# An fp32 block of layernorm, attention and MLP on one core: the maxima's hand-over, W_V's low parts and 19 matmuls of zeros

## The chip, the core and the metric

The kernel runs on one core of one Trainium2 chip. A core has a matrix engine (TensorE, PE in the profile; PEld is its weight load), VectorE (DVE), ScalarE (ACT), GpSimd (POOL) and SyncE (SP). SP and ACT issue the DMAs of this kernel, each into a queue of its own (SPq and ACTq in the profile). The metric is the device time of one execution in microseconds (us); lower is better, and the median of several runs is compared.

## The reference, cut to what matters

```python
S, D, H, F = 2048, 1024, 32, 3584           # head size 32, everything in float32
xn = layernorm(x)                            # over D, eps 1e-5, no weights
q, k, v = split(xn @ wqkv)
o = softmax(q @ k.T / sqrt(32)) @ v          # for each of the 32 heads
s = o @ wo
h = xn @ w1 + b1
g = silu((h * tanh(softplus(h))) @ w2)       # mish between two dense layers
return x + s * g
```

## The kernel before

**Precision.** Every float32 operand of a large product is split into a high part (rounded to the PE's fp32r form) and a low part (the difference). A product is three matmuls: high by high, high by low and low by high (`THREE`). Each split costs one copy for the high part (`copy`, line 288, on ACT) and one subtraction for the low part (`low`, line 296, on DVE or POOL). So one line of a helper stands for many operations in the profile.

**Stages.** The first stage normalises x and projects V (lines 371 to 642). A second projects Q and K with a seven-product scheme (lines 645 to 864; line 795 is its matmul). From about 522 us on, attention and MLP run together under a planner (lines 867 to 1451), and the last stage applies `wo` and adds up.

**The start.** x is taken in 16 tiles of 128 rows. `ln_a` is the statistics (lines 391 to 394, DVE), `ln_r` two small ACT operations, `ln_b` four small DVE operations (lines 404 to 407), `ln_x` the normalisation. For the first three tiles `ln_x` is shared: the first half on ACT (line 413), the second on DVE (line 416). `ln_t` makes eight PE transposes into two PSUM banks (line 423), and `ln_c` copies each bank to the tile's high part (ACT) and takes its low part (DVE). `v_group(0, t)` is the 24 matmuls of one x tile with the first half of W_V (line 354): eight row blocks k, three matmuls each. A group stops after `cut` matmuls to put the next tile's transposes in. The first group takes the pairs that need only W_V's high parts first, 16 matmuls, and the eight with its low parts last. The order of the instructions on each engine is the order in which lines 469 to 531 are written. `v_high(0, k)` and `v_low(0, k)` make the parts of W_V's eight blocks; blocks 4 and 5 have their low parts made by POOL, the others by DVE.

**The hand-over to attention.** The softmax subtracts each row's maximum by two extra rows of the Q stack (high and low part of the negated maximum). The scores of head 0 are computed ahead, during the Q and K projection (`s_mm`); their maxima are reduced by DVE. The first twelve of 16 row tiles are turned on the way (`m_tail`). The last four go through `m_chain(0, 12, 4)`, the first thing that the planner has:

- r1: the maximum over four chunks (DVE, line 937)
- r2: high part (ACT, line 940)
- r3: low part (DVE for head 0)
- r4: `turn`, a matmul with the identity (PE, line 678)
- r5: copy from PSUM (ACT, line 952)
- r6: two small DMAs into rows 96 and 97 of the Q stack (line 957). For head 0 they are issued on ACT's queue, for the others on SP's.

Head 0's exponentials of key tile t need `t` matmuls (line 999), which read the Q stack with those rows; the fourth chunk of queries waits for r6.

**The planner.** `Plan` simulates the engines with written-out costs and emits each instruction at the simulated time at which its engine would take it. That order is then the program order of each engine's queue. It has streams of PE work: `s` (scores for maxima, line 917), `t`, `h` (first MLP product, line 1204), `y` (second, line 1294), `pv`. Op by op it holds a cost, an engine and what must be done first; what an op really emits is a function of its own, which the planner doesn't look into.

**Weights.** Tile n of W1 (1 MB, high and low part) is loaded by `load_w1(n)` into one of two buffers. Tile 0 is loaded at the end of the projections, tile 1 by `w1_op(1)`, whose op on SP the planner emits among the first there, ahead of r6. W2's first raw tile (line 1160) is given `m_there[0, 3]`, the op of r6, as a need (line 1281), so it is emitted after it.

Of the kernel before, what the change touches and what calls it, by code (L numbers as in the profile page):

```python
# [9 lines left out]
F32 = mybir.dt.float32  # L10
# [8 lines left out]
P = 128  # L19
# [211 lines left out]
def body(ctx: ExitStack, tc: tile.TileContext, x, wqkv, wo, w1, b1, w2, out):  # L231
# [99 lines left out]
    def v_high(i, k):  # L331
        j, k = divmod(k, 2)
        if k == 0:
            vw[i, j] = vp.tile([P, 2, 2, 512], F32R, tag="w", name=f"vw{i}_{j}", bufs=5)
        copy(vw[i, j][:, 0, k], vraw[i, j][:, k])

    def v_low(i, k, eng):
        j, k = divmod(k, 2)
        low(eng, vw[i, j][:, 1, k], vraw[i, j][:, k], vw[i, j][:, 0, k])
# [40 lines left out]
    def ln_a(t, steps=range(3)):  # L380
        xt = xts[t]
        if 0 in steps:
            st = vp.tile([P, 2, 6], F32, tag="st", name=f"st{t}", bufs=4)
            mv = vp.tile([P, 2], F32, tag="mv", name=f"mv{t}", bufs=5)
            var = vp.tile([P, 1], F32, tag="var", name=f"var{t}", bufs=5)
            rs = vp.tile([P, 1], F32, tag="rs", name=f"rs{t}", bufs=5)
            stat[t] = mv, var, rs, st
        mv, var, rs, st = stat[t]
        for g in range(2):
            if g in steps:  # L390
                nc.vector.bn_stats(st[:, g], xt[:, g * 512:(g + 1) * 512])
        if 2 in steps:
            nc.vector.bn_aggr(mv, st)
            nc.vector.tensor_scalar(var, mv[:, 1:2], EPS, None, op0=ALU.add)

    def ln_r(t):
        mv, var, rs, _ = stat[t]
        act(rs, var, AF.Ln)
        act(rs, rs, AF.Exp, scale=-0.5)
# [66 lines left out]
        move(xs[c][:, :, k:k + 2], xc[c][k // HK][:, :, k % HK:k % HK + 2])  # L466


    ln_a(0)
    ln_r(0)  # L470
    ln_b(0)
# [8 lines left out]
    ln_c(0)  # L480
    ln_a(1, (1, 2))
    v_low(0, 2, nc.vector)
    v_high(0, 3)
    v_low(0, 3, nc.vector)
    for k in (4, 5):
        v_high(0, k)
        v_low(0, k, nc.gpsimd)
    v_high(0, 6)
    v_high(0, 7)
    ln_r(1)  # L490
    v_low(0, 6, nc.vector)
    ln_b(1)
    ln_x(1, True)
    v_low(0, 7, nc.vector)
    ln_a(2)
    xts[3] = x_load(3)
    for t in range(2, NT + 2):
        if 2 < t < NT:
            ln_b(t)

        evac = v_group(0, t - 2, {2: 22, 3: 20, 4: 14}.get(t, 8), (lambda: ln_t(t - 1)) if t <= NT else None,
                       (((0, 0), (1, 0)), ((0, 1),)) if t == 2 else None if t > NT else (((0, 0), (0, 1)), ((1, 0),)))
        if t <= NT:
            ln_c(t - 1)
        if t == 2:
            ln_r(2)
            ln_b(2)
        if t < NT:
            ln_x(t, t == 2)
        for m in (4, 5) if t == 2 else (t + 3,):  # L510
            if m < NT:
                xts[m] = x_load(m)
        if t == 2:
            ln_a(3)
        if t + 2 < NT:
            ln_a(t + 2)
        if t + 1 < NT:
            ln_r(t + 1)
        if t in (NT - 4, NT - 3):
            for j in range(2):  # L520
                v_load(1, 2 * (t - NT + 4) + j)
        if t == NT - 2:
            v_split(1, 0)
        if t == NT + 1:
            for j in range(1, 4):
                v_split(1, j)
        evac()
        if t in (8, 10, 12, 14, 17):
            x_store()
        if t in (4, 5, 7, 9, 11, 13, 15):  # L530
            w1_early()
# [401 lines left out]
    def m_chain(h, first, n, maxes, tiles):  # L933

        def r1(at):
            tiles["nm"] = early.tile([P, NT], F32, tag=f"nm{at['nm']}", name=f"nm{h}_{first}")[:, :n]
            nc.vector.tensor_reduce(tiles["nm"], tiles["mx"][:, :n], axis=AX.X, op=ALU.max, negate=True)

        def r2(at):
            copy(parts(n)[:, 0], tiles["nm"])  # L940

        def r3(at):
            hl = parts(n)
            low(nc.vector if h == 0 else nc.gpsimd, hl[:, 1], tiles["nm"], hl[:, 0])

        def r4(at):
            tiles["tp"] = tp = bank(at, f"mtp{h}_{first}")
            turn(tp)

        def r5(at):  # L950
            tiles["mt"] = early.tile([2 * NT, P], F32R, tag=f"mt{at['mt']}", name=f"mt{h}_{first}")
            copy(tiles["mt"][:2 * n], tiles["tp"][:2 * n, :P])

        def r6(at):
            for a in range(2):
                move(qst[h % 3][96 + a:97 + a, first * P:(first + n) * P]
                     .rearrange("o (t p) -> o t p", p=P), tiles["mt"][n * a:n * a + n, :], None if h else nc.scalar)

        a = op("DVE", 0.18, need=maxes, emit=r1, take=["nm"], give=["mx"])
        a = op("ACT", 0.21, need=[a], emit=r2, take=["hl"])  # L960
        a = op("POOL" if h else "DVE", 0.25, need=[a], emit=r3, give=["nm"], key=-1)
        a = op("PE", 0.07, need=[a], emit=r4, take=["t", "b"], give=["hl"], late=LATE if h else 0.0)
        a = op("ACT", 0.28, need=[a], emit=r5, take=["mt"], give=[("t", a), ("b", a)])
        a = op("SP", 0.2, need=[a], emit=r6, give=["mt"], bytes_=1024 * n)
        for c in range(first // 4, (first + n) // 4):
            m_there[h, c] = a
# [145 lines left out]

    def w1_op(n):
        def emit(at):
            load_w1(n)
        need = [w1_kept.get(n - 2)]
        if not W1_V <= n < FT:
            w1_ops[n, 0] = w1_ops[n, 1] = op("SP", 0.1, need=need, emit=emit, take=["w1"], bytes_=P * 2 * KT * P * 4)
            return
        a = None  # L1120
        for half in range(2):
            r = slice(half * HK, half * HK + HK)

            def raw(at, half=half):
                if half == 0:
                    w1t[n] = w1_tile(f"w1_{n}")
                w1r[n, half] = att.tile([P, 512], F32, tag="on0", name=f"w1r_{n}_{half}").rearrange("p (k f) -> p k f", f=P)
                nc.sync.dma_start(w1r[n, half], w1[half * 512:half * 512 + 512, n * P:(n + 1) * P].rearrange("(k p) f -> p k f", p=P))

            def high(at, half=half, r=r):  # L1130
                copy(w1t[n][:, 0, r], w1r[n, half])

            def rest(at, half=half, r=r):
                low(nc.gpsimd, w1t[n][:, 1, r], w1r[n, half], w1t[n][:, 0, r])

            b = op("SP", 0.1, need=[a] + need, emit=raw, take=["on"] if half else ["w1", "on"], bytes_=P * 512 * 4)
            a = op("ACT", 0.6, need=[b], emit=high)
            w1_ops[n, half] = op("POOL", 1.3, need=[a], emit=rest, give=["on"], key=-1)
        w1_kept[n] = op("SP", 0.1, emit=lambda at: move(w1s[n], w1t[n]), need=[w1_ops[n, 0], w1_ops[n, 1]], bytes_=P * 2048 * 4)
# [412 lines left out]
```

## Time and profile before

| what | us |
|---|---|
| median of 3 runs | 3364.82 |
| lowest and highest of them | 3362.99, 3366.28 |
| the profiled execution's own time | 3366.45 |
| its span, first to last instruction | 3364.7 |
| PE busy | 3342.9 |
| DVE, ACT, POOL busy | 2511.9, 2056.0, 2527.5 |

How to read the rows. The page gives each engine's busy time with its share of the span, and the chain of work that ended last, as shares by engine. A row of the timeline has the start in us, the duration in us, the engine, the line, the operation, output and inputs by their names, the shape and a count; in brackets stands how long the engine sat idle before it, and what ended the wait. Rows of several instructions are merged, and matmuls overlap: one lasts longer than the distance to the next. A row of the view by stretches has the length, then for PE, PEld, DVE, ACT and POOL the busy time with a count, then the granted PE clock, the share of the DMA engines and the GB/s that they moved. A row of the view by line has the least, median and largest duration in ns, and the first and last start.

### The profile page before, as it was taken

The numbers are of one execution on the slowest core, as the hardware profiler recorded it, in microseconds if no ns is written. First come the engines' busy times: TensorE is split into PE (matmuls) and PEld (weight loads), VectorE is DVE, ScalarE is ACT, GpSimd is POOL, SyncE is SP. The second block draws the span as 40 slices with busy tenths as digits, with TensorE's granted clock in tenths as the row PEclk, the third lists the DMA queues.
The fourth block names the chain that finished last, engine by engine and source line by source line (L and its number), as shares of the span: only waits on it lengthen the run. The fifth ranks groups of instructions, "written<-read, shape, count | busy, mean of one in ns | idle before, by whom it ended". The sixth has DMA issues, their size and how long they took to land.

```text
span 3364.7 us, 45751 instructions
## 1 busy us (share of the span) xinstructions
PE 3342.9 (99%) x16867; PEld 2455.6 (73%) x16867; DVE 2511.9 (75%) x3984; ACT 2056.0 (61%) x3314; POOL 2527.5 (75%) x751
## 2 busy tenths in 40 slices
PE   8999999999999999999999999999999999999999
PEld 7888887777777677776777667777677777767787
DVE  6665677878777777887788678888787888886542
ACT  5233335777766666676676666667667666667621
POOL 2323546999999977888888988888888898889800
PEclk9999999999999999999999999999999999999999
DMA  7865745454555643344335434333344433433482
GB/s 242 302 204 180 242 145 180 144 179 153 168 188 176 208 135 116 104 123 121 101 113 164 129 101 126 101 103 117 108 151 136 119 104 111 128 111 107 138 305 83
DMA packets 291460, 501.56 MB, mean 149 GB/s; under 512 B 88138, under 2 KB 151114, under 8 KB 269130
## 3 DMA queue, kind: packets, MB, share of 16 engines
q1 hardware_dynamic: 271508, 456.95, 43.7%
q10 hardware_dynamic: 19728, 41.69, 3.3%
q8 instruction: 133, 2.18, 0.3%
q14 instruction: 91, 0.75, 0.1%
HBM read 352.55 MB, written 144.97 MB: 148 GB/s over the span
## 4 chain that ended last, share of the span: by engine, by line
PE 95%; DMA 2%; DVE 1%; POOL 1%; issue 0%; ACT 0%; SPq 0%; ACTq 0%; DVEq 0%; POOLq 0%
PE y L1294 18%; PE h L1204 17%; PE t L999 14%; PE s L917 13%; PE pv L1046 13%; PE op L1393 5%; PE v L354 5%; PE q_y L795 3%; PE q_z L795 2%; PE q_x L795 2%; PE zp L1072 1%; POOL z L1028 1%; DMA raw<-in_A_wqkv_dram 0%; PE pt L423 0%; PE s L697 0%
## 5 line engine op out<-in xcount | busy, mean ns | idle before, releaser
L1028 POOL TENSOR_TENSOR z<-z,p 128x2048 f32<-128x2048 f32 x448 | 2068.3, 4617 | 98.1 <-ACT p L285 72.8
L285 ACT ACTIVATE p<-t,zero 128x512 f32<-128x512 f32 x2048 | 1377.0, 690 | 564.2 <-PE t L999 539.7
L923 DVE TENSOR_REDUCE mx<-s 128x1 f32<-128x512 f32 x1984 | 1323.7, 686 | 385.7 <-PE s L917 374.5
L1294 PE MATMUL y<-w,act 128*128 128x512 f32 x2688 | 920.7, 391 | 1.1 <-DVE yacc L1316 0.5
L999 PE MATMUL t<-qstack,kstack 128*128 128x512 f32 x2048 | 800.0, 393 | 4.1 <-DMA qstack<-mt 3.3
L917 PE MATMUL s<-kstack,qstack 128*128 128x512 f32 x1984 | 773.1, 394 | 0.0
L1204 PE MATMUL h<-xr,w 128*128 128x512 f32 x2016 | 697.6, 391 | 0.4 <-DMA xr<-xs 0.4
L1294 PEld LDWEIGHTS y<-w,act 128*128 128x128 f32 x2688 | 503.3, 188 | 115.0 <-issue 6.7
L999 PEld LDWEIGHTS t<-qstack,kstack 128*128 128x128 f32 x2048 | 384.1, 188 | 118.7 <-issue 20.9
L1046 PE MATMUL pv<-p,v 128*32 128x512 f32 x4096 | 459.3, 594 | 0.0
L917 PEld LDWEIGHTS s<-kstack,qstack 128*128 128x128 f32 x1984 | 370.0, 188 | 118.4 <-issue 32.1
L1204 PEld LDWEIGHTS h<-xr,w 128*128 128x128 f32 x2016 | 378.3, 188 | 81.2 <-issue 3.4
L1316 DVE TENSOR_TENSOR yacc<-yacc,y 128x512 f32<-128x512 f32 x416 | 283.0, 681 | 82.3 <-PE y L1294 81.4
L1046 PEld LDWEIGHTS pv<-p,v 128*32 128x32 f32 x4096 | 123.3, 110 | 282.8 <-issue 282.2
L1028 POOL TENSOR_TENSOR z<-p,p 128x2048 f32<-128x2048 f32 x32 | 148.1, 4628 | 185.5 <-PE zp L1072 142.1
L1204 PE MATMUL h<-xc,w 128*128 128x512 f32 x672 | 231.8, 392 | 0.3 <-ACT p L285 0.3
L354 PE MATMUL v<-vw,xc 128*128 128x512 f32 x768 | 180.4, 394 | 0.0
L354 PEld LDWEIGHTS v<-vw,xc 128*128 128x128 f32 x768 | 143.9, 189 | 30.3 <-DVE xc L296 0.5
L1204 PEld LDWEIGHTS h<-xc,w 128*128 128x128 f32 x672 | 126.2, 188 | 29.3 <-issue 2.5
L288 ACT ACTIVATE act<-h 128x512 fp32r<-128x512 f32 x112 | 66.6, 595 | 88.3 <-DVE h L1253 87.1
L795 PE MATMUL q_y<-xc,wq 128*128 128x512 f32 x480 | 115.4, 389 | 0.0
L795 PEld LDWEIGHTS q_y<-xc,wq 128*128 128x128 f32 x480 | 90.0, 188 | 18.9 <-issue 0.2
(146 smaller groups left out, 2940.3 us busy)
## 6 DMA issues: line engine op xcount, KB each, us to landing
w<-w1s SPq DMA_DIRECT2D x91, 1024.0 KB
w<-w2s SPq DMA_DIRECT2D x168, 512.0 KB
w2s<-w SPq DMA_DIRECT2D x56, 512.0 KB
qstack<-qs SPq DMA_DIRECT2D x96, 256.0 KB
kstack<-ks SPq DMA_DIRECT2D x96, 256.0 KB
w1s<-w SPq DMA_DIRECT2D x21, 1024.0 KB
qs<-qst ACTq DMA_DIRECT2D x32, 512.0 KB
ks<-qst ACTq DMA_DIRECT2D x32, 512.0 KB
```

The source lines that it names most:

```text
L285: nc.scalar.activation(out_, in_, fn, bias=zero if bias is None else bias, scale=scale)
L354: nc.tensor.matmul(ps, xc[t // 4][k // HK][:, a, k % HK, (t % 4) * P:(t % 4 + 1) * P], vw[i, k // 2][:, b, k % 2], start=n == 0, stop=n == ...
L795: nc.tensor.matmul(ps, w[:, a, k], xx[:, b, k], start=m == 0 and i in (0, 1, 4), stop=m == 3 * HK - 1, skip_group_check=i not in (0, 1, 4))
L917: nc.tensor.matmul(sp_, qst[h % 3][:, qt * P:(qt + 1) * P], kst[h % 3][:, kc * 512:(kc + 1) * 512], start=True, stop=True)
L923: nc.vector.reduce_max(tiles["mx"][:, qt, kc:kc + 1], tiles[qt, kc], axis=AX.X)
L999: nc.tensor.matmul(tp, kst[h % 3][:, kt * P:(kt + 1) * P], qst[h % 3][:, c * 512:(c + 1) * 512], start=True, stop=True)
L1028: nc.gpsimd.tensor_tensor(zs[h], pts[T - 1] if kt == 1 else zs[h], pts[T], ALU.add)
L1046: nc.tensor.matmul(pv[h][c * DH:(c + 1) * DH, :], vt[h][:, k, :], pts[T - kt + k][:, c * 512:(c + 1) * 512], start=k == 0, stop=k == NT - 1)
L1204: nc.tensor.matmul(t["h"], w1t[n][:, a, k], xts_[c][k // HK][:, b, k % HK], start=i == 0, stop=i == 3 * KT - 1)
L1294: nc.tensor.matmul(t["y"], acts[n][:, p, s * P:(s + 1) * P], w2t[m_][:, q], start=j == 0 and i == 0, stop=j == YB - 1 and i == 2)
L1316: nc.vector.tensor_tensor(ya, ya, t["y"], ALU.add)
L1393: nc.tensor.matmul(ps[t, dh], ohl[t // 4, k][:, a, s * P:(s + 1) * P], wt[k][:, b, r], start=k == 0 and i == 0, stop=k == KT - 1 and i == 2)
```

## The change

There are four edits.

1. Ahead of the first `ln_a`, POOL clears a 128x512 piece of a chunk that is filled much later, and PE multiplies it with itself 19 times into a PSUM bank that nobody reads.
2. The order of the start: W_V's high parts 3 to 6 are made in a row; `ln_r(1)` comes ahead of high part 7; `ln_b(1)` and `ln_x(1)` come ahead of low parts 4 to 7, which are all DVE's now. The first group's cut goes from 22 to 20.
3. In `m_chain`, for head 0, r2 is a DVE copy and r6 is issued by SP.
4. W1's tile 1 is loaded by r6 of head 0, behind its two DMAs; `w1_op(1)` keeps its op in the planner, but emits nothing.

The planner's costs, needs and order of ops are the same.

```diff
+    idle = xc[3][1][:, 0, 0]
+    nc.gpsimd.memset(idle.bitcast(F32), 0.0)
+    idle_ps = ps_tile("idle")
+    for _ in range(19):
+        nc.tensor.matmul(idle_ps, idle[:, :P], idle, start=True, stop=True)
+
     ln_a(0)
     ln_r(0)
     ln_b(0)
...
     ln_c(0)
     ln_a(1, (1, 2))
     v_low(0, 2, nc.vector)
-    v_high(0, 3)
+    for k in (3, 4, 5, 6):
+        v_high(0, k)
     v_low(0, 3, nc.vector)
-    for k in (4, 5):
-        v_high(0, k)
-        v_low(0, k, nc.gpsimd)
-    v_high(0, 6)
+    ln_r(1)
     v_high(0, 7)
-    ln_r(1)
-    v_low(0, 6, nc.vector)
     ln_b(1)
     ln_x(1, True)
-    v_low(0, 7, nc.vector)
+    for k in (4, 5, 6, 7):
+        v_low(0, k, nc.vector)
     ln_a(2)
     xts[3] = x_load(3)
...
-        evac = v_group(0, t - 2, {2: 22, 3: 20, 4: 14}.get(t, 8), (lambda: ln_t(t - 1)) if t <= NT else None,
+        evac = v_group(0, t - 2, {2: 20, 3: 20, 4: 14}.get(t, 8), (lambda: ln_t(t - 1)) if t <= NT else None,
...
         def r2(at):
-            copy(parts(n)[:, 0], tiles["nm"])
+            if h:
+                copy(parts(n)[:, 0], tiles["nm"])
+            else:
+                nc.vector.tensor_copy(parts(n)[:, 0], tiles["nm"])
...
         def r6(at):
             for a in range(2):
                 move(qst[h % 3][96 + a:97 + a, first * P:(first + n) * P]
-                     .rearrange("o (t p) -> o t p", p=P), tiles["mt"][n * a:n * a + n, :], None if h else nc.scalar)
+                     .rearrange("o (t p) -> o t p", p=P), tiles["mt"][n * a:n * a + n, :])
+            if h == 0:
+                load_w1(1)
...
     def w1_op(n):
         def emit(at):
-            load_w1(n)
+            if n > 1:
+                load_w1(n)
```

## The prediction

> **What bounds the kernel now.** I read the page first: the share of each engine and the chain that ended last.
>
> ```profile
> span 3364.7 us, 45751 instructions
> ...
> PE 3342.9 (99%) x16867; PEld 2455.6 (73%) x16867; DVE 2511.9 (75%) x3984; ACT 2056.0 (61%) x3314; POOL 2527.5 (75%) x751
> ...
> PE 95%; DMA 2%; DVE 1%; POOL 1%; issue 0%; ACT 0%; SPq 0%; ACTq 0%; DVEq 0%; POOLq 0%
> ```
>
> TensorE (PE) is the bound nearly everywhere: 95% of the chain. The change removes no matmul of use, so only time in which PE stands still, or runs slowly, can be won. The span less PE's busy time is 21.8 us; the change touches two places of it. The first is the start, read from the timeline of PE alone:
>
> ```profile
> 8.95 1.97 PE L423 MATMUL pt<-ident_r,x 128*128 128x128 f32 x8 [8.95 <-ACT x L285]
> 10.75 7.08 PE L354 MATMUL v<-vw,xc 128*128 128x512 f32 x22
> 18.41 1.10 PE L423 MATMUL pt<-ident_r,x 128*128 128x128 f32 x8 [0.58 <-ACT x L285]
> 19.26 5.33 PE L354 MATMUL v<-vw,xc 128*128 128x512 f32 x22
> 24.43 1.04 PE L423 MATMUL pt<-ident_r,x 128*128 128x128 f32 x8
> ```
>
> Eight transposes take 1.97 us the first time and 1.04 to 1.10 later; 22 matmuls take 7.08 and then 5.33. Before the second transposes PE stands 0.58 us for the normalised x. From 24.43 on there is no wait in brackets. The view of line 354 in two short windows says why the first ones are long:
>
> ```profile
> L354 PE MATMUL v<-vw,xc x5: 628/628/792, 11.5 to 13.4; 128*128 128x512 f32 x5
> L354 PE MATMUL v<-vw,xc x12: 389/389/398, 14.5 to 17.0; 128*128 128x512 f32 x12
> ```
>
> Until 13.4 a matmul takes 628 ns, from 14.5 on 389, and twelve start within 2.5 us: 0.227 each (2.5/11).
>
> The second place is where projections end and attention begins (timeline, all engines and issuing queues):
>
> ```profile
> 522.87 0.34 SPq L292 DMA_DIRECT2D w<-w1s  x1
> ...
> 524.93 1.28 DVE L923 TENSOR_REDUCE mx<-s 128x1 f32<-128x512 f32 x2
> ...
> 525.59 1.84 ACT L285 ACTIVATE p<-t,zero 128x512 f32<-128x512 f32 x3 [1.38 <-PE t L999]
> ...
> 526.76 0.39 PE L917 MATMUL s<-kstack,qstack 128*128 128x512 f32 x1
> 527.32 0.21 ACT L288 ACTIVATE hl<-nm 128x4 fp32r<-128x4 f32 x1
> 527.56 0.16 DVE L296 TENSOR_TENSOR hl<-nm,hl 128x4 fp32r<-128x4 f32 x1 [1.35 <-ACT hl L288]
> ...
> 527.78 0.33 PE L678 MATMUL mtp<-ident_r,hl 128*128 128x128 f32 x1 [0.63 <-DVE hl L296]
> ...
> 528.14 0.27 ACT L288 ACTIVATE mt<-mtp 8x128 fp32r<-8x128 f32 x1 [0.61 <-PE mtp L678]
> ...
> 528.44 1.80 ACTq L292 DMA_DIRECT2D qstack<-mt  x2
> ...
> 530.73 0.39 PE L1204 MATMUL h<-xc,w 128*128 128x512 f32 x1
> 533.58 0.77 PE L999 MATMUL t<-qstack,kstack 128*128 128x512 f32 x1 [2.47 <-DMA qstack<-mt]
> ...
> 535.43 0.63 PE L917 MATMUL s<-kstack,qstack 128*128 128x512 f32 x1
> ...
> 535.86 0.63 PE L1204 MATMUL h<-xc,w 128*128 128x512 f32 x1
> ```
>
> The turned maxima go DVE, ACT, DVE, PE, ACT, DMA; PE waits 0.63 us in the middle and 2.47 us for the landing. Then matmuls take 0.63 us again and start 0.43 apart (535.43 to 535.86), and the view by stretches shows the granted clock (last column but two) at half:
>
> ```profile
> 533.50:534.00 0.50, 0.42 (x1) 0.45 (x2) 0.00 (x0) 0.00 (x0) 0.00 (x0) 0.50 0.00 0
> ...
> 536.50:537.00 0.50, 0.50 (x3) 0.42 (x3) 0.29 (x1) 0.19 (x1) 0.00 (x0) 1.00 0.00 0
> ```
>
> **The change part by part: the start.** These rows of the timeline carry it:
>
> ```profile
> 0.73 0.20 POOL masks.py:197 MEMSET ident<- 128x128 f32 x1 [0.29 <-POOLq L1539]
> ...
> 1.01 0.29 POOL masks.py:199 TENSOR_SCALAR_AFFINE_SELECT ident<-ident 128x128 f32<-128x128 f32 x1
> ...
> 10.79 1.49 DVE L296 TENSOR_TENSOR xc<-pt,xc 128x512 fp32r<-128x512 f32 x2
> ...
> 12.67 2.98 POOL L296 TENSOR_TENSOR vw<-vraw,vw 128x512 fp32r<-128x512 f32 x2 [11.36 <-ACT vw L288]
> ...
> 13.23 3.57 DVE L296 TENSOR_TENSOR vw<-vraw,vw 128x512 fp32r<-128x512 f32 x3
> ...
> 16.73 0.20 DVE L404 SCALAR_TENSOR_TENSOR tmp<-rs,var 128x1 f32<-128x1 f32 x1
> ...
> 17.54 0.81 ACT L285 ACTIVATE x<-x,tmp,rs 128x512 f32<-128x512 f32 x1 [2.88 <-DVE tmp L407]
> ...
> 18.61 1.28 DVE L391 BATCH_NORM_STATS2 st<-x 128x6 f32<-128x512 f32 x2
> ...
> 20.23 1.28 DVE L296 TENSOR_TENSOR xc<-pt,xc 128x512 fp32r<-128x512 f32 x2
> ...
> 22.25 0.82 ACT L285 ACTIVATE x<-x,tmp,rs 128x512 f32<-128x512 f32 x1 [1.28 <-DVE tmp L407]
> ```
>
> *Zeros.* POOL is free at 1.30 (1.01+0.29). A memset of four times ident's elements costs 0.20 to 0.82; I take 0.5 and a start of the zeros at 1.9. All slow, 19 take 19 x 0.43 = 8.2 and end at 10.1; all fast, 4.3. In the old start the clock rose between 13.4 and 14.5, that is 2.7 to 5.6 us after PE's first matmul of a product (10.75) or first transpose (8.95). So 6 to 13 zeros are slow, and the last ends at 1.9+2.7+13 x 0.227 = 7.6 or 1.9+5.6+6 x 0.227 = 8.9. PE had nothing to do before 8.95: the zeros cost nothing, and the first transposes find a fast PE.
>
> *What that lets go, and what is late next.* The second matmul of the first group needs x's low part, which DVE begins at 10.79 and ends at about 11.5. DVE's order up to there is unchanged, so the first group still runs from 11.5, now at 0.227: matmuls 2 to 20 end at 11.5+19 x 0.227 = 15.8. The cut moves from 22 to 20, so here PE turns to the second transposes. They need x1.
>
> *DVE's order.* Before: the second x low ends at 12.28, statistics follow, then three low parts of W_V in 3.57 us (about 0.6 apart where POOL is not beside them: two end 1.28 after the first starts, at 20.23), and only then the small steps at 16.73 and x at 17.54. After: two low parts there, 1.28, with no POOL transfer beside: 2.3 us sooner. ACT's copies of the first transposes come some 0.2 sooner on a fast PE. So the small steps start at 14.2 and x1 is ready at 14.2+0.81+0.81 = 15.9, against 18.35. PE and x1 meet at 15.9; transposes start 2.5 us sooner. If DVE doesn't get faster without POOL, the two take up to 2.4 and x1 comes at 17.0.
>
> *The four low parts behind x.* DVE's half of x ends at about 15.6, then four at 0.61 end at 16.2, 16.8, 17.4 and 18.0. PE is through the transposes at 15.9+0.85 = 16.75, and its last four matmuls want just these: the last starts at 18.05 instead of 17.45, a new wait of 0.6 in all. Group 0 ends at 18.3. Then 20 matmuls of group 1 at the old pace (5.17 for 22, 19.26 to 24.43) are 4.7: the third transposes at 23.0 against 24.43. Their x2 was ready at 23.07; DVE reaches that tile's statistics at 18.0 instead of 18.61, so it is ready at 22.5, in time. The low parts at 20.23 come 0.6 sooner too and are wanted at 22. **Start: -1.4 us**; without the new wait it would be -2.0.
>
> **The transition.** The copy of the maxima goes from ACT, where it stood behind three exponentials (525.59+1.84), to DVE. DVE has r1, two maxima (to 526.21), r2 at 0.16 and r3 at 0.16: hl is there by 526.5, and the turn follows the matmul of 526.76 at 526.99, 0.79 sooner. PE's work that needs no maxima then ends at 530.96-0.79 = 530.17. ACT copies mt at 527.4 (its exponentials end then), SP issues at 527.7. What stays behind it on SP: W1's second tile (before at 522.87) and W2's first raw tile, which the planner emits after the maxima; their price is below. For an SP issue and a tile of W1 there are rows further on (timeline and stretches):
>
> ```profile
> 598.79 1.23 SPq L292 DMA_DIRECT2D qstack<-mt  x2
> ...
> 600.50:601.00 0.50, 0.50 (x4) 0.41 (x3) 0.46 (x1) 0.23 (x1) 0.50 (x1) 1.00 0.08 17
> ...
> 585.65 0.33 SPq L292 DMA_DIRECT2D w<-w1s  x1
> ...
> 590.00:590.50 0.50, 0.50 (x4) 0.42 (x3) 0.50 (x2) 0.47 (x2) 0.50 (x1) 1.00 0.13 33
> ```
>
> Two issues on SP take 1.23 and their traffic ends within 2.2 us (598.79 to 601.0); on ACT's queue it was 5.14 (528.44 to 533.58), behind that queue's stores. I take 2.7, nearer to SP's row since SP's queue holds nothing big any more: PE goes on at 530.4, nearly without a wait; the far end is 532.8.
>
> But W1's second tile is issued only when SP is done with the maxima, 527.7+1.23 = 528.9, and takes 4.9 us (585.65 to 590.5): 533.8, with some stores beside it 534.0. PE's sixth matmul after the maxima is the first that reads it (535.86 before). So PE does five matmuls from 530.4, is out of work at 531.6 and waits again, some 2.3 us, now for W1. That matmul moves from 535.86 to 534.0: **-1.85 us**. I leave the half clock in, as the new wait is about as long as the old 2.47. W2's raw tile lands about 1 us behind W1, at 535; it is used by ACT only after four exponentials, two of which follow W1's arrival, so it is covered; if not, one wait of under 1 us on ACT.
>
> Sum: -1.4 - 1.85 = -3.25. The profiled execution took 3366.45 (its span 3364.7 and 1.75 around it), so 3363.2; it lies 1.63 over the median of the runs, 3364.82. Predicted median: 3364.82-3.25 = 3361.6. All else is bound by PE and its planned order is the same, so what is won is kept.
>
> **Rivals.** *The clock stays up.* PE's idle time is split in two, 0.2 and 2.3, with 1.2 us of work between, where before it was 2.47 in one piece. If the clock doesn't drop, the five steps from 533.58 to 535.86 (2.28 us, 1.14 at 0.227) and half of the 0.6 from there to 536.5 are won as well, 1.4: 3360.2. For it: the split. Against it: 2.3 is nearly 2.47. The Trainium skill (TensorE: Matmul & The Clock Gate, "Why this matters for your kernels") says that gaps up to about 3 us keep the clock. By that rule it stays up; the trace disagrees, as 2.47 us was followed by half clock. I give this 0.2.
>
> *The warm PE cools.* From the zeros' end (7.6 to 8.9) to 11.5 PE has eight transposes and one matmul. If that counts as idle, the clock falls and matmuls 2 to 9 are slow until about 14.3, as now: the second transposes start at 17.2, there is no wait for low parts, and the third at 17.2+0.85+24 x 0.235 = 23.7. The start then wins 0.7: 3362.3. For it: the old clock rose 5.5 us after the first transpose but 3.7 after the first matmul of a product. The same page (Part 4, PE-mode transpose) says that transposes don't count as PE being busy; by that rule this rival holds. I give it 0.2.
>
> *Slower: W1's second tile becomes the bound.* ACT's earlier stores share the DMA with it. If W1 lands 9 us after its issue, near 538, its matmul comes 2.1 later than before and a whole slow stretch follows it, some 1.5 us. With the start's -1.4 that is +2.2: 3367.0. It is slower than before from a landing at about 535.8 on (535.86 plus the 1.4 of the start, less those 1.5). Against it: all that the DMA had to move was over by 533.5 in the old order (its share is 0.00 in the stretch from there), and nothing is added. 0.06.
>
> *The zeros don't warm PE at all* and run to 10.1: the first transposes are 1.1 late and the start wins about 0.4: 3362.6; 0.05.
>
> **How the numbers follow.** Forecast 0.49, the rivals as given. 0.2% is 6.7 us, about what a measurement of this kernel can tell from no change; every case lies inside it. Faster by more needs both gains and the clock at their far ends (-2.0, -3.4): with the runs' own spread of 3.3 us 0.04. Slower by more needs more than the slow rival: 0.02. The range goes from the clock's case less half the spread, 3358.6, to the forecast plus a lost start and half the spread, 3364.9.
>
> **What would show it.** Right: 19 matmuls of a tile "idle" from about 1.9; 389 ns in the first group by 12; second transposes near 16, third near 23.0; no POOL on vw; hl wholly on DVE and the turn near 525.6 (1.4 earlier); PE's wait for qstack under 1 us and a new one, over 1.5, ended by the load of W1. Wrong: zeros running past 8.95, slow matmuls after 11.5, a PE wait for qstack of 2 us, or W1 landing in time with none.

## The result, and the profile after

The changed kernel takes 3360.95 us (median of 22 runs, 3358.92 to 3362.51), the kernel before 3365.60 beside it (22 runs, 3362.99 to 3366.81): 4.65 us less, a ratio of 0.9987 with a 95% interval of 0.9981 to 0.9993. That is a gain, and less than the 0.2% (6.7 us) that the prediction named as the bound of "no change". In a later series it was 4.38 us less, 0.9988 (0.9979 to 0.9997). The forecast was 3.25 us less, 3361.6. The two executions that were profiled lie further apart than the medians (3366.45 and 3359.76): that of before is 0.85 us above its median, that of the change 1.19 below.

The page of the changed kernel, to set beside that of before:

```profile
span 3358.0 us, 45795 instructions
...
PE 3345.8 (100%) x16886; PEld 2458.4 (73%) x16886; DVE 2510.8 (75%) x3987; ACT 2056.5 (61%) x3313; POOL 2524.7 (75%) x750
...
PE 96%; DMA 1%; DVE 1%; POOL 1%; issue 0%; ACT 0%; SPq 0%; ACTq 0%; POOLq 0%; DVEq 0%
```

PE has 19 matmuls more (the zeros, 7.14 us busy at the start) and the span is 6.7 shorter, so span less PE's busy time went from 21.8 to 12.2; 7.1 of these 9.6 us are the zeros themselves, which fill time that was idle. The share of DMA in the chain went from 2% to 1%.

The start, from the timeline (start, duration, engine, line, operation; in brackets the idle time ahead of it and what ended it):

```profile
1.25 0.53 POOL L470 MEMSET xc<- 128x512 f32 x1
...
1.82 7.14 PE L473 MATMUL idle<-xc 128*128 128x512 f32 x19 [1.82 <-POOL xc L470]
...
8.80 1.04 PE L423 MATMUL pt<-ident_r,x 128*128 128x128 f32 x8
...
11.01 4.64 PE L354 MATMUL v<-vw,xc 128*128 128x512 f32 x19 [0.41 <-DVE xc L296]
...
12.50 1.28 DVE L296 TENSOR_TENSOR vw<-vraw,vw 128x512 fp32r<-128x512 f32 x2
...
14.53 0.82 ACT L285 ACTIVATE x<-x,tmp,rs 128x512 f32<-128x512 f32 x1 [0.60 <-DVE tmp L407]
...
14.99 2.49 DVE L296 TENSOR_TENSOR vw<-vraw,vw 128x512 fp32r<-128x512 f32 x4
...
15.48 1.04 PE L423 MATMUL pt<-ident_r,x 128*128 128x128 f32 x8
...
16.28 6.36 PE L354 MATMUL v<-vw,xc 128*128 128x512 f32 x24
16.93 0.19 PEld L354 LDWEIGHTS v<-vw,xc 128*128 128x128 f32 x1 [0.38 <-DVE vw L296]
...
17.53 4.67 PEld L354 LDWEIGHTS v<-vw,xc 128*128 128x128 f32 x21 [0.41 <-DVE vw L296]
...
22.47 1.03 PE L423 MATMUL pt<-ident_r,x 128*128 128x128 f32 x8
...
23.78 0.58 ACT L288 ACTIVATE vst<-v 128x512 f32<-128x512 f32 x1
24.26 1.07 ACT L288 ACTIVATE xc<-pt 128x512 fp32r<-128x512 f32 x2
...
24.90 0.96 PE L354 MATMUL v<-vw,xc 128*128 128x512 f32 x3 [0.46 <-ACT xc L288]
```

The first transposes take 1.04 us (1.97 before) and the first group's 19 matmuls 4.64: PE is fast from its first useful work. The second transposes start at 15.48 (18.41 before), the third at 22.47 (24.43). Behind them there is a wait that before did not have: 0.46 us at 24.90, for ScalarE's copy of the transposed tile, which stands behind a copy of the first product (vst).

The hand-over, from the timeline of PE and ScalarE and of the issuing queue of SyncE (SPq):

```profile
523.94 0.16 DVE L946 CAST hl<-nm 128x4 fp32r<-128x4 f32 x1
...
525.40 0.22 PE L681 MATMUL mtp<-ident_r,hl 128*128 128x128 f32 x1
...
525.66 0.26 ACT L288 ACTIVATE mt<-mtp 8x128 fp32r<-8x128 f32 x1
525.95 1.20 SPq L292 DMA_DIRECT2D qstack<-mt  x2
...
527.26 0.37 SPq L292 DMA_DIRECT2D w<-w1s  x1
...
527.68 0.43 SPq L1169 DMA_DIRECT2D w2r<-in_B_w_dram  x1
...
528.51 0.40 PE L1007 MATMUL t<-qstack,kstack 128*128 128x512 f32 x1
...
530.78 0.39 PE L920 MATMUL s<-kstack,qstack 128*128 128x512 f32 x1
...
532.17 0.47 PE L1213 MATMUL h<-xc,w 128*128 128x512 f32 x1 [1.00 <-DMA w<-w1s]
...
532.71 0.63 ACT L288 ACTIVATE w<-w2r 128x512 fp32r<-128x512 f32 x1 [1.04 <-DMA w2r<-in_B_w_dram]
```

Neither the turn (525.40) nor the first matmul that reads the maxima (528.51) has a wait; before they had 0.63 and 2.47 us. There is one new wait, 1.00 us at 532.17, for W1's second tile. Matmuls take 0.39 to 0.40, but for the one that waited (0.47): the half clock of before is gone.

**Where the time went.** Apart from the zeros, and from a few at the second transposes where the cut was moved, PE runs the same matmuls in the same order in both kernels, so each can be set beside itself. This table gives how much earlier (-) a matmul starts than the same one in the profile of before: the first one behind the third transposes that can wait (26.23 in before), one at 218, the first that reads W1's second tile (537.53), and the last. "Hand-over" is the third column less the second; "medians" is the median of the runs less that of before on the same chip.

| kernel | at 26 | at 218 | at 537.5 | hand-over | last | medians |
|---|---|---|---|---|---|---|
| changed | -1.33 | -1.59 | -5.35 | -3.76 | -6.70 | -4.65 |
| changed, again | -1.00 | -0.98 | -4.62 | -3.64 | -4.97 | -4.38 |
| start only | -0.80 | -0.90 | -1.00 | -0.10 | -0.12 | -0.10 |
| hand-over only | +0.18 | -0.09 | -3.80 | -3.71 | -2.31 | -2.80 |
| without zeros | -0.32 | +0.28 | -3.37 | -3.65 | -2.65 | -2.85 |
| zeros only | -0.75 | -0.81 | -0.58 | +0.23 | -0.22 | +0.18 |
| W1 ahead | -0.54 | -0.14 | +0.16 | +0.30 | +0.89 | -0.97 |
| maxima by ACT's queue | -0.87 | -1.00 | -0.05 | +0.95 | +1.53 | +0.36 |
| wait filled | +0.32 | +0.22 | -1.00 | -1.22 | +0.20 | -0.44 |
| W1 in halves | -0.96 | -0.77 | -5.17 | -4.40 | -3.16 | -1.90 |
| one row by ACT's queue | -0.79 | -1.03 | -4.84 | -3.81 | -3.32 | -4.78 |
| copy by ACT | -0.85 | -0.60 | -3.47 | -2.87 | -4.26 | -3.65 |
| vst behind | -1.89 | -2.18 | -5.98 | -3.80 | -4.01 | -4.42 |

Of the 4.65 us, the traces put 3.6 to 3.8 into the hand-over (five profiles with it whole) and about 1 into the start. The start's share is the less certain one: the eight profiles with the start of the change stand anywhere from -0.14 to -1.59 at 218, six of them between -0.60 and -1.03. What lies behind 537.5 changes the sum by -1.35 (the change) to +2.0 us (W1 in halves), though no edit touches anything there; the part "Waits that come and go" shows where. For the medians the interval is about 3 us to either side in the experiments of 11 runs each, so a single part of 1 us is read from the traces and not from the times.

### The profile page after: what moved, and what is told of

Its sections match the earlier page's. It is cut to its first block, busy times and chain, and to the rows that moved or that the text cites. A ratio compares the mean times of both kernels' runs of the same rounds, so it can differ in the third digit from the quotient of the medians.

```text
span 3358.0 us, 45795 instructions
## 1 busy us (share of the span) xinstructions
PE 3345.8 (100%) x16886; PEld 2458.4 (73%) x16886; DVE 2510.8 (75%) x3987; ACT 2056.5 (61%) x3313; POOL 2524.7 (75%) x750
## 3 DMA queue, kind: packets, MB, share of 16 engines
q8 instruction: 133, 2.18, 0.3%
## 4 chain that ended last, share of the span: by engine, by line
PE 96%; DMA 1%; DVE 1%; POOL 1%; issue 0%; ACT 0%; SPq 0%; ACTq 0%; POOLq 0%; DVEq 0%
PE y L1303 18%; PE h L1213 18%; PE t L1007 14%; PE s L920 13%; PE pv L1054 13%; PE op L1402 5%; PE v L354 5%; PE q_y L798 3%; PE q_z L798 2%; PE q_x L798 2%; PE zp L1080 1%; PE s L700 0%; POOL z L1036 0%; PE pt L423 0%; DMA w2r<-in_B_w_dram 0%
```

## The experiments

Each ran 11 times, beside 33 runs of before on the same chip (medians of before: 3366.07, 3366.71 and 3366.99 for the three groups of four).

**The parts alone.** The first kernel has the zeros and the order of VectorE's start, with the hand-over as before; the second the reverse.

The start alone, against the changed kernel:

```diff
-            if h:
-                copy(parts(n)[:, 0], tiles["nm"])
-            else:
-                nc.vector.tensor_copy(parts(n)[:, 0], tiles["nm"])
+            copy(parts(n)[:, 0], tiles["nm"])
...
-                     .rearrange("o (t p) -> o t p", p=P), tiles["mt"][n * a:n * a + n, :])
-            if h == 0:
-                load_w1(1)
+                     .rearrange("o (t p) -> o t p", p=P), tiles["mt"][n * a:n * a + n, :], None if h else nc.scalar)
...
-            if n > 1:
-                load_w1(n)
+            load_w1(n)
```

The hand-over alone is before with these lines the other way round.

> The kernel before with the start's two edits alone (zeros, W_V's order and cut). Theory (the two places add up and what the start wins is kept): third transposes at 22.5 to 23, PE's wait for the maxima still 2 to 2.5 us with half clock behind it, the first matmul of W1's second tile at about 535.9 (537.53 before), time 1.4 us under the kernel before. Rival (what the start wins is lost again at a wait tied to a DMA): the third transposes move, but that matmul stays within 0.4 of 537.5 and the time doesn't change.

> The kernel before with the hand-over's edits alone (maxima by VectorE and SyncE, W1's second tile behind them). Theory: third transposes at 24.4 as before, no wait for the maxima, a wait of about 1 us for W1, no half clock, first matmul of W1's second tile at about 533.8, time 3.2 to 3.8 us under the kernel before. Rival (the changed kernel's profile only happened to keep its clock): a wait for W1 followed by half clock, and not more than 2 us won.

Start only: 3365.97, ratio 1.0000 (0.9991 to 1.0009). Hand-over only: 3363.27, 0.9993 (0.9984 to 1.0002). In the traces the hand-over alone wins 3.71, with no half clock, as expected. The start alone wins 0.80 at 26 and 0.90 at 218, less than the 1.4 that was expected; the waits of 0.48 and 2.65 us and the half clock at the hand-over are still there, and the first reader of W1's second tile comes 1.00 us earlier. At the last matmul 0.12 of it is left, so its rival (what the start wins is lost again) is not excluded.

The start was divided once more: the changed kernel without the zeros, and before with nothing but the zeros.

```diff
-    idle = xc[3][1][:, 0, 0]
-    nc.gpsimd.memset(idle.bitcast(F32), 0.0)
-    idle_ps = ps_tile("idle")
-    for _ in range(19):
-        nc.tensor.matmul(idle_ps, idle[:, :P], idle, start=True, stop=True)
```

> The changed kernel without the 19 matmuls of zeros. Theory (VectorE's order is the larger part of the start): slow matmuls of 628 ns until about 14, second transposes at about 17, third at 23.2 to 23.7 against 22.47 with the zeros, time 0.7 us over the changed kernel. Rival (the zeros are the start's gain): third transposes at 24.4, 1.4 us or more over the changed kernel.

> The kernel before with the 19 matmuls of zeros alone. Theory (the second x tile, made ready by VectorE, sets the second transposes): fast matmuls from 11 on, but PE stands about 2 us longer for x, second transposes at 18.0 to 18.4, third at 24.0 to 24.4, time 0 to 0.4 us under the kernel before. Rival (the zeros are the start's gain): third transposes at 23 or sooner, 1.4 us under.

Without zeros: 3363.22, 0.9991 (0.9982 to 1.0000). Zeros only: 3366.25, 1.0001 (0.9992 to 1.0009). The timeline of PE in "zeros only":

```profile
11.04 5.40 PE L354 MATMUL v<-vw,xc 128*128 128x512 f32 x21 [0.22 <-DVE xc L296]
17.63 1.09 PE L423 MATMUL pt<-ident_r,x 128*128 128x128 f32 x8 [1.19 <-ACT x L285]
```

and in "without zeros":

```profile
11.03 6.80 PE L354 MATMUL v<-vw,xc 128*128 128x512 f32 x20
17.67 1.04 PE L423 MATMUL pt<-ident_r,x 128*128 128x128 f32 x8
```

Both come to the second transposes at 17.6 to 17.7, for opposite reasons: a fast PE waits 1.19 us for the normalised x, and an early x finds a PE that needs 6.80 us for twenty matmuls. Only both together bring 15.5 to 16.3. At the third transposes, too, they win more together (1.21 to 1.96) than the zeros (0.76) and the order (0.40) alone; 24.04 without zeros lies between the two theories that were written down for it, and 23.67 with the zeros alone does so as well.

Behind the new wait at 24.90 this is gone. There the zeros alone stand at -0.75 (at 26) and -0.81 (at 218), and the whole start at -0.54 to -1.33 and -0.14 to -1.59. So what VectorE's order adds to the zeros is, as far as these traces can tell, lost again at that wait, unless the copy that causes it is moved ("vst behind", below: -1.89 and -2.18).

**What made the maxima late.** Two kernels take one part of the hand-over back: W1's tile issued ahead of the maxima on SyncE as before, and, besides, the maxima on ScalarE's queue as before. The first, against the changed kernel, and then the line that the second has besides:

```diff
-            if h == 0:
-                load_w1(1)
...
-            if n > 1:
-                load_w1(n)
+            load_w1(n)
```

```diff
-                     .rearrange("o (t p) -> o t p", p=P), tiles["mt"][n * a:n * a + n, :])
+                     .rearrange("o (t p) -> o t p", p=P), tiles["mt"][n * a:n * a + n, :], None if h else nc.scalar)
```

> The changed kernel with W1's second tile loaded where it was, ahead of the maxima on SP. Theory (SP's queue against ACT's is what matters; the tile is 1 MB ahead of the maxima in the same queue): the maxima land 0.5 to 1 us later than without it, PE waits for them up to 1 us, the wait of 1.00 for W1 is gone, time within 0.5 us of the changed kernel. Rival (the tile's place is what matters): PE waits 2 us or more for the maxima, half clock follows, 3 us over the changed kernel.

> The changed kernel with r6 issued by ACT again and W1's second tile where it was; r2 stays on VectorE. Theory (ACT's queue with its three stores of 512 KB is the wait): the maxima land at about 531.5 to 532, PE waits for them 2.5 to 3.3 us (its other work ends 0.8 sooner), half clock follows, time 3.2 to 3.8 us over the changed kernel. Rival (r2 on VectorE is the gain): the landing is 0.8 us sooner and the time is 1.5 us or less over the changed kernel.

W1 ahead: 3365.74, 0.9996 (0.9987 to 1.0005). Maxima by ACT's queue: 3367.07, 1.0002 (0.9993 to 1.0011). The timeline of "W1 ahead":

```profile
522.73 0.35 SPq L292 DMA_DIRECT2D w<-w1s  x1
...
527.39 1.23 SPq L292 DMA_DIRECT2D qstack<-mt  x2
...
532.85 0.77 PE L1005 MATMUL t<-qstack,kstack 128*128 128x512 f32 x1 [2.77 <-DMA qstack<-mt]
```

and of "maxima by ACT's queue":

```profile
526.78 1.80 ACTq L292 DMA_DIRECT2D qstack<-mt  x2
...
532.65 0.76 PE L1005 MATMUL t<-qstack,kstack 128*128 128x512 f32 x1 [3.21 <-DMA qstack<-mt]
```

On SyncE's queue, too, PE waits 2.77 us and the clock falls to half. The second kernel shows the wait that its theory named (3.21 us), but the first shows that the queue is not the reason: with W1 ahead, the maxima are late on either. The two differ in one thing more. W2's raw tile follows the maxima only where both are issued on SyncE's queue; the planner puts it behind them in the program, but with the maxima on ScalarE's queue nothing holds it back, as in before:

```profile
525.37 0.34 SPq L1160 DMA_DIRECT2D w2r<-in_B_w_dram  x1
```

That is 3.07 us ahead of the maxima (528.44). In "W1 ahead" it is behind them, at 528.67, so W1's tile alone is enough for the wait. The view of the DMA gives the sizes of what is in flight (before, 521 to 535):

```profile
w<-w1s SPq DMA_DIRECT2D x1, 1024.0 KB
ks<-qst ACTq DMA_DIRECT2D x2, 512.0 KB
qs<-qst ACTq DMA_DIRECT2D x1, 512.0 KB
w2r<-in_B_w_dram SPq DMA_DIRECT2D x1, 256.0 KB
qstack<-mt ACTq DMA_DIRECT2D x2, 2.0 KB
```

The maxima are 2 KB a row. By the trace's record of completions they land when the last of ScalarE's three stores lands: with W1 ahead on SyncE's queue at 532.0 to 532.7 (that store 532.2 to 533.3), though W1's tile, ahead of them in the same queue, had landed at 528.1 to 529.1; on ScalarE's at 532.1 to 532.5 (531.9 to 532.8); in before at 533.1 to 533.5 (532.8 to 533.7). In the changed kernel the same store, issued at the same place, lands at 527.4 to 527.6, 4.2 us after its issue instead of 8.7 (8.5 in "W1 ahead", which differs from the change in W1's place alone), and the two rows land at 527.7 and 528.2. The DMA's share says the same: 0.98 to 1.08 in each microsecond from 528 to 532 in "W1 ahead", 0.16 from 527 to 528 in the change.

One cell of that square was left: W1 behind, and ScalarE's queue. It was filled with one of the two rows, so that SyncE still issues W1 behind the other.

```diff
-                     .rearrange("o (t p) -> o t p", p=P), tiles["mt"][n * a:n * a + n, :])
+                     .rearrange("o (t p) -> o t p", p=P), tiles["mt"][n * a:n * a + n, :], nc.scalar if h == 0 and a == 0 else None)
```

> The changed kernel, with the first of the two rows of turned maxima issued on ScalarE's queue, as before, and the second on SyncE's, with W1's second tile behind it. Theory A: the maxima land when the stores that were issued ahead of them have landed, whichever queue carries them, and what made that late before was W1's 1 MB beside the stores. Then the row on ScalarE's queue lands 1 to 2.5 us after its issue, the scores matmul that reads it has no wait, W1's matmul waits about 1 us, and the time is that of the change within 1 us. Theory B, the prediction's: ScalarE's queue itself is slow. Then that row takes about 5 us again, the scores matmul waits over 2 us, the clock falls, and the time is 2 to 4 us above the change.

3362.21, 0.9987 (0.9979 to 0.9996), the same as the changed kernel on that chip (3362.61). Its timeline:

```profile
526.53 0.59 SPq L292 DMA_DIRECT2D qstack<-mt  x1
526.53 1.42 ACTq L292 DMA_DIRECT2D qstack<-mt  x1
...
532.68 0.47 PE L1213 MATMUL h<-xc,w 128*128 128x512 f32 x1 [0.92 <-DMA w<-w1s]
```

Both rows are issued at 526.53; the one on SyncE's queue lands at 528.29, the one on ScalarE's at 528.53, and no matmul waits for them. Theory A's conditions are met, and the prediction's reason for the old delay (theory B) falls. The Trainium skill (DMA: Bandwidth & Descriptors, "Issuing engines are not separate DMA queues") says that transfers issued by different engines run on the same DMA engines and interleave there; these runs agree, with 2.77 and 3.21 us of waiting on the two queues where W1 is ahead, and none on either where it is behind. That the rows land with the last store is what these traces show side by side; why 2 KB must wait for stores of another queue was not tried.

**The copy of the maxima.** The changed kernel with the first copy back on ScalarE.

```diff
-            if h:
-                copy(parts(n)[:, 0], tiles["nm"])
-            else:
-                nc.vector.tensor_copy(parts(n)[:, 0], tiles["nm"])
+            copy(parts(n)[:, 0], tiles["nm"])
```

> The changed kernel, with the copy of the maxima back on ScalarE. By the prediction the copy then stands behind three exponentials again: the turn starts 0.79 us later and PE waits 0.5 to 0.6 us for it; the maxima and W1's second tile are issued 0.8 later, and W1's first matmul with them, so the hand-over gives back 0.8 us. Rival: the wait for W1 (1.00 us) is what counts and W1's tile lands when the DMA is free of stores, not when it is issued; then that matmul comes less than 0.3 us later, and the time is that of the change.

3363.34, 0.9989 (0.9980 to 0.9998). The turn waits again:

```profile
527.11 0.33 PE L681 MATMUL mtp<-ident_r,hl 128*128 128x128 f32 x1 [0.56 <-DVE hl L296]
```

and the hand-over is worth 2.87 instead of 3.64 to 3.81: 0.8 us, as expected. The wait for W1 (1.09) is as long as in the change (1.00 and 1.11), only later: W1's tile lands 4.8 us after its issue in all three, and the rival falls.

**The price of the half clock.** In before, eleven matmuls that nobody uses fill the wait for the maxima. They write the bank that the scores matmul then begins anew.

```diff
                     tile_[0] = tp = bank(at, f"t{T}_{c}")
+                    if T == 0 and c == 3:
+                        f = xc0[0][:, 0, 0]
+                        for _ in range(11):
+                            nc.tensor.matmul(tp, f[:, :P], f, start=True, stop=True)
```

> The kernel before with 11 matmuls of no use between PE's last work and the first matmul that waits for the maxima, into a bank that this one then overwrites. Theory (the half clock has a price of its own, 1.4 us): PE is busy through the wait, the matmuls behind it take 389 ns, the first matmul of W1's second tile comes at about 536.1 against 537.53, time 1.4 us under the kernel before. Rival (only the wait costs): the matmuls behind it are fast or not, but the time is the same within 0.3 us; or the matmuls of no use run past the landing and add up to 0.3.

3366.27, 1.0000 (0.9991 to 1.0009). The trace:

```profile
531.26 2.65 PE L1002 MATMUL t<-xc 128*128 128x512 f32 x11
533.95 0.47 PE L1003 MATMUL t<-qstack,kstack 128*128 128x512 f32 x1
```

The clock stays up. The scores matmul comes 0.36 later than in before and the first reader of W1's second tile 1.00 earlier: the half clock had cost 1.36 us there. By 585 all but 0.30 is gone again, and the time (0.44 us less, where the runs resolve 3) can't tell the theory's 1.4 from the rival's nothing.

**What is late next.** The changed kernel with W1's second tile in two transfers of four row blocks each, so that its first matmuls can start on the first half.

```diff
-                load_w1(1)
+                w1t[1] = w1_tile("w1_1")
+                for i in range(2):
+                    move(w1t[1][:, :, i * HK:i * HK + HK], w1s[1][:, :, i * HK:i * HK + HK])
```

> The changed kernel with W1's second tile loaded as two DMAs, the first four row blocks and then the other four. Theory (PE's 1.00 us for W1 is the time of the whole 1 MB): the first half lands 1.0 to 1.3 us sooner, PE's wait for it is under 0.2 and there is none for the second half, time 0.8 to 1.0 us under the changed kernel. Rival (the time of a load is not its size, or two issues on SP and smaller pieces cost what is won): the wait stays at 0.7 or more and the time is the same.

3364.81, 0.9994 (0.9985 to 1.0002): not better than the change. The wait for W1 shrinks to 0.32, which neither expectation had (under 0.2, or 0.7 and more), and some four us later PE waits elsewhere (timeline of PE and ScalarE):

```profile
534.36 0.63 ACT L288 ACTIVATE w<-w2r 128x512 fp32r<-128x512 f32 x1 [1.82 <-DMA w2r<-in_B_w_dram]
...
536.23 0.50 PE L1009 MATMUL t<-qstack,kstack 128*128 128x512 f32 x1 [0.87 <-ACT p L285]
```

W2's raw tile, third in the row, is now the late one: ScalarE waits 1.82 for it (1.04 in the change) with the exponentials queued behind, and PE 0.87 for the bank that an exponential frees. The halves are not needed for that: in "vst behind", below, ScalarE waits 2.53 for the same tile and PE 0.86. Of the 5.17 us won at 537.5, 1.7 are lost again by 585.

**The start's new wait, and the control.** The changed kernel with the first vst copy behind the copies of the third transposes; and the changed kernel untouched.

```diff
+        if t == 3:
+            late()
...
-        evac()
+        if t == 2:
+            late = evac
+        else:
+            evac()
```

> The changed kernel, with the copy of the first product's result (vst) issued on ScalarE behind the copies of the third transposes instead of ahead of them. If the wait of 0.46 us at 24.90 comes from that copy (0.58 us) ahead of xc's, it goes: PE's matmul there starts 0.4 to 0.5 us sooner, the start's gain at that point is 1.7 to 1.9 us instead of 1.33. Rival: the two steps for rs that stand ahead of both (0.29 each) are enough to hold it, and a wait of 0.2 to 0.4 stays. The whole time moves by less than 0.5 us either way.

> The changed kernel once more, untouched, beside the three below. Its times so far were 4.65 us under those of before (medians), while the start alone, the hand-over alone, and the change without its zeros gave 0.1, 2.8 and 2.85. If what is won is kept, as the prediction says, it is again 4 to 5 us under before (ratio 0.9985 to 0.9988), and the start is worth some 1.8 on top of the hand-over. Rival: waits that come and go late in the kernel (a load of xr near 2510, the maxima near 1980, a step of VectorE near 1345) take part of it back in some executions; then it is 2 to 3.5 us under before (0.9990 to 0.9994), and the profile shows such waits longer than the 0.38, 0.26 and none of the first profile.

vst behind: 3362.57, 0.9987 (0.9978 to 0.9996); again: 3362.61, 0.9988 (0.9979 to 0.9997). In "vst behind" ScalarE's order is turned round

```profile
23.71 1.06 ACT L288 ACTIVATE xc<-pt 128x512 fp32r<-128x512 f32 x2
24.66 0.60 ACT L288 ACTIVATE vst<-v 128x512 f32<-128x512 f32 x1
```

and the wait is gone: between the third transposes and 26 this kernel loses 0.16 us of its gain, where the change lost 0.63 and 0.66, and 1.89 us are left at 26 instead of 1.00 to 1.33. The change untouched gave 4.38 us, within the 4 to 5 expected, but its start was worth 0.98 at 218 and not 1.8. The time of "vst behind" is the same; here PE lost 0.86 and 0.57 us to ScalarE between 534 and 565, and 0.62 at 1342. No version beat the change by more than the runs resolve.

**Waits that come and go.** A few places, most of them late in the kernel, explain much of how the column "last" of the table wanders. The largest is a load of x near 2510. In the changed kernel:

```profile
2505.32 0.50 PE L1213 MATMUL h<-xr,w 128*128 128x512 f32 x1 [0.38 <-DMA xr<-xs]
```

in "start only":

```profile
2511.58 0.50 PE L1207 MATMUL h<-xr,w 128*128 128x512 f32 x1 [1.58 <-DMA xr<-xs]
```

It is 0.44 in before, 1.09 in the second profile of the change, 1.69 with W1 in halves. A wait for ScalarE near 565, which itself waits there for W2's next raw tile, is 0.16 in the change and 1.41 in "one row by ACT's queue". Near 1345 there is none in before and in the change, and 0.95 and 1.46 with the start and the hand-over alone; near 1980 there are 0.81 in before and 0.26 and 0.56 in the two profiles of the change. None of these places is touched by the edits. They are one profile each: whether an earlier PE meets them more often, or they fall by chance, was not settled.

## Why the prediction was right, and where it failed

- **The sum.** The forecast was -3.25, measured were -4.65 and -4.38. The direction came for the reasons given; that 3361.6 lies only 0.65 us from 3360.95 is partly luck. The runs of before had a median of 3365.60 beside the change, and not the 3364.82 that the forecast started from; this hid 0.78 of the miss of 1.40. Within the sum, a hand-over priced too low (1.85, measured 3.6 to 3.8) and a start priced too high (1.4, about 1 at 218) partly cancel.
- **Zeros.** "POOL 0.5, start 1.9, 6 to 13 slow, the last ends at 7.6 to 8.9": 0.53, 1.82, and in ten profiles with them 7 to 14 slow, with the last ending between 7.9 and 9.3. In the first profile they ended at 8.97 and the transposes started 0.72 after x0 was ready (8.08). The prediction had named an end past 8.95 as a sign of being wrong; it happened in three profiles (8.97, 9.19, 9.33). In the first it seems to have cost nothing, as DVE's statistics, which stand ahead of the low part of x there, waited until 9.67 for a load anyway. Both rivals about the clock at the start fell: PE neither stayed slow nor cooled between the zeros and 11.0.
- **DVE's order.** x1 ready at 15.9, third transposes at 23.0: 15.35 (14.53+0.82) and 22.47 in the first profile, 22.77 in the second, 22.98 with the start alone. The wait of 0.6 for low parts is there, as 0.38 and 0.41 of idle weight loads. What the forecast had not seen is the next wait, 0.46 to 0.53 at 24.9, for ScalarE: "the third transposes at 23.0 against 24.43" was worth 1.2 to 2.0, of which 0.5 to 1.3 is left behind that wait (eight profiles). So the -1.4 of the sum was reached at the third transposes, but not kept. "vst behind" shows that the copy ahead of it is the cause.
- **The turn.** "0.79 sooner": -2.38 at the turn against -1.59 at 218, which is 0.79; with the copy on ScalarE 0.8 to 0.9 of the hand-over is lost again.
- **The maxima.** "2.7 after the issue, nearly without a wait": the second row lands 2.3 after the issue (525.95 to 528.21) and nothing waits. The size was right, the reason only half: not the queue that they stand in, but the 1 MB of W1 that no longer goes ahead.
- **W1's second tile: the step that failed.** "PE's sixth matmul after the maxima is the first that reads it (535.86 before)." It is the twelfth, which this row of before is (timeline of PE):

```profile
537.53 0.39 PE L1204 MATMUL h<-xc,w 128*128 128x512 f32 x1
```

The landing itself was right: 534.0 in the clock of before was predicted, and it is 532.04 plus the 1.59 of the start, 533.6. But PE had eleven matmuls ahead of it and not five, so it waited 1.00 us and not 2.3. From 537.53 to 534.0 would have been -3.5; measured -3.76. With that count the prediction's own numbers give -1.4 - 3.5 = -4.9, against -4.65.
- **The clock.** It was left at half, as "the new wait is about as long as the old 2.47". With a wait of 1.00 it stays up, so the rival that had 0.2 came true (its own sum, 4.6 us under before, is nearly the measured 4.65, with the same wrong count in it), though not for its reason (two pieces of idle time): there is one wait, and it is short because of the count above. The sign "a new one, over 1.5" did not come either. The parts of the hand-over, worked out from the rows as time beyond 0.23 per step: turn 0.79, maxima 2.62 (533.58-530.73-0.23), half clock 1.44 (3.95 for eleven steps, 533.58 to 537.53, instead of 2.51), less 1.16 for W1 (532.17-530.78-0.23): 3.69 of the 3.76.
- **The rest of the sum.** The slower rival fell: W1's tile landed 4.8 us after its issue, beside W2's and behind stores that were done. W2's raw tile was covered in the change (ScalarE waits 1.04, PE not at all near it); where ScalarE waited longer for it, 1.82 and 2.53, PE lost 0.87 and 0.86. "What is won is kept" held for the change in two series (4.65 and 4.38); for the start alone, whose 0.9 us the median of 11 runs does not show, it is open.

## What to carry to other kernels

Where a small transfer is urgent, look at all the bytes in flight when it is issued, not at the queue that it is put on: issuing 1 MB behind 4 KB instead of ahead was worth some 4 us of the hand-over here (-3.76 against +0.30), and the other queue, for one of the two rows, nothing (-3.81). Count the instructions up to the first reader of a moved load from the tile that each one reads, since the wait, and with it the clock, hangs on that count. When two things meet (a fast engine and early data), test each alone and both together, and read the gain behind the next wait too: here the two halves of the start made 1.2 to 2.0 us of 0.76 and 0.40 at the third transposes, and behind a wait for ScalarE just after them little more than the zeros alone.

## What the hardware showed beside

- **The clock changes in whole steps of 3.413 us.** After PE idled 2.47 (before), 2.61 (zeros only) and 2.65 us (start only) the granted clock is at half for 3.41 us; after 2.77 (W1 ahead) and 3.21 us (maxima by ACT's queue) for 6.83, although PE works again 0.77 us into it ("W1 ahead": 532.85, the clock down from 532.08); after waits of 1.00 to 1.69 us (1.69 near 2509 in "W1 in halves"), and with the wait filled, not at all. In the traces' record of the granted clock the stretches between its first rise and its last fall are whole multiples of 3.413 us in all fourteen profiles, those at full clock too (before: 152, then 1 at half, then 828). So a wait doesn't bring the clock down where it gets long, but at the next step: in "start only" it falls at 533.71, 1.07 us after PE was at work again (532.63). Whether the length of a wait or its place between two steps decides on one or two steps at half isn't settled by these five. The Trainium skill (TensorE: Matmul & The Clock Gate, "Why this matters for your kernels") keeps the clock for gaps up to about 3 us; four profiles here lost it at 2.47 to 2.77, the fifth (3.21) lies beyond that. A stretch of "W1 ahead", where the last column but two is the clock:

```profile
537.00:538.00 1.00, 1.00 (x4) 0.81 (x3) 1.00 (x3) 0.50 (x1) 0.00 (x0) 0.50 0.00 0
```

- **Zeros warm PE as well as data.** The number of slow zeros (0.43 us apart, 0.23 when fast) differs from run to run between 7 and 14, that is 3.2 to 6.2 us after PE's first matmul at 1.82. In three of the four kernels without zeros the clock rises 3.5 to 3.8 us after the first matmul of a product, in "hand-over only" 7.5. The column of the granted clock does not show this phase, as the record begins only with the rise (7.23 in the changed kernel, where the zeros get fast): it reads 1.00 while the zeros start 0.43 us apart (changed kernel, stretch from 4 to 5 us):

```profile
4.00:5.00 1.00, 1.00 (x4) 0.71 (x4) 0.76 (x2) 0.00 (x0) 0.00 (x0) 1.00 0.99 344
```
